# A seven-product down projection allowed earlier in the first pass, with new costs in the planner that orders all engines

## The chip, the cores and the metric

One core of a Trainium2 chip runs the whole kernel. The metric is the device time of one execution in microseconds (us). A core has five engines that run side by side and wait for each other through semaphores: TensorE (PE in the profile, its weight loads PEld), VectorE (DVE), ScalarE (ACT), GpSimd (POOL) and SyncE (SP), which here only issues DMAs. SBUF is the on-chip memory, PSUM the banks that TensorE writes into.

## The reference

The input x has 8192 tokens of 448 features. The reference normalizes each token, sends the result down two branches, and joins them:

```python
    x = A_x
    xn = _layernorm(x, axis=-1)
    s = _A_ref(xn, A_w1, A_b1, A_w2, A_b2)
    g = _silu(_B_ref(xn, B_w_gate, B_w_up, B_w_down))
    return x + s * g
```

Branch A (`_A_ref`) is a real FFT over the 8192 tokens, a two-layer complex MLP on each frequency in four blocks of 112 features, a soft threshold, and the inverse FFT. Branch B (`_B_ref`) is a gated feed-forward network (FFN), `(_gelu(x @ w_gate) * (x @ w_up)) @ w_down`, with 448 features in, 1792 hidden and 448 out. All arithmetic has to hold float32-like accuracy, so the kernel splits each float32 operand into two float16 halves, high and low, and uses three matmuls (high x high, high x low, low x high) for one product.

## The kernel before

**Two passes of the FFN.** The 14 hidden blocks of 128 do not fit at once. A first pass (p = 0) takes blocks 0 to 7, a second (p = 1) blocks 8 to 13. Each pass runs over 16 chunks of 512 tokens (`NG`, `ffn`, `chunk`). Chunks 0 and 1 of the first pass are done in a plain way at the start (`plain`, `down`). The partial result of the first pass goes to DRAM as `prt` and is read back in the second.

**One chunk.** `chunk(p, i)` works on pairs of hidden blocks, four pairs in the first pass and three in the second. Gate and up projection of a pair use a Strassen-like scheme of seven products (`unit`, `product`, steps a1 to a7) with operands that were combined before: the token side is prepared by stage 1 (`chunk1`, `factors`), goes through DRAM as `xts` and comes back transposed as `xta` and `xtb`; the weight side is prepared by `gu_comb`. After them comes the down projection, in one of two forms:

- *Plain* (`down`, `ended`): for each of the four tiles of 128 tokens and each of the 8 hidden blocks three matmuls of 448 columns, 96 in all; one ACT eviction per token tile.
- *Seven products* (`down2`, `prod2`, `add2`, `ended2`): the same Strassen-like scheme on pairs of hidden blocks, halves of the features and pairs of token tiles: seven products for each of four pairs, in two halves, with three matmuls of 224 columns each. It needs sums and differences of the hidden values (`sums` inside `unit`), and a right-hand side of combined down weights. Evictions add into a tile that an earlier product has filled. Half of this chunk's down projection is issued inside the next chunk (`state["tail"]`), between its first products.

The flag `state["seven"]` chooses. It is set at the start of a chunk, once and for good, when `state["products"]` is there and, in the first pass, the chunk number is at least 9. Setting it starts `factors_in(0)`, which loads the combined down weights from DRAM (`dsp`) into `dw`, into parts of `wt` and into `state["right"]`.

**Where "products" comes from.** `weights()` runs the preparation of weights in the background: first the blocks of the first pass (`gu_loads`, `gu_block`, `gu_split`, then `gu_combs`), then `room()`, which gives back the buffers, then four tasks `factor0(j)`. Each loads 256 rows of the down weights into the one remaining buffer of the ring `WS`, builds seven combinations and stores them to `dsp[0]`. `state["products"]` is set 3 us after the last of them is planned to land. Then follow the blocks of the second pass (`far_tile`), its down weights and the weights of the MLP (`prep_mlp`).

**Phases beside the FFN.** Stage 1 of the FFT is in `chunk1`, which also makes the FFN's input; its chunks are released every `DT` us from `T1` on (`first`). Phase 2 (`phase2`, `group`) starts when stage 1 and all preparation are done, and spreads 64 groups up to `END2` = 1450 us. Phase 3 (`phase3`, `load3`, `tiles3`) does the last inverse step and the output. It starts when phase 2 has stored everything. For chunks whose gate was stored to DRAM by then (`gsp`), it loads the gate into one of two buffers `g2`, multiplies, adds x and stores the output. Chunks that come later take the inverse step themselves (`gate_bank`, `gate`).

**The order.** Nothing here is ordered by hand, and nothing by the compiler. The kernel contains a planner, `Pace`: every step is a Python generator, a model clock decides which generator continues, and the instructions go into the engines' queues in that order. `cost` gives a duration for each instruction, `start` the earliest time, `note` and `ready` what was read and written when. `STEPS` corrects the model by time: in each row stand the start time, a limit for engines that are busy ahead (used by `clear`), an allowance for loads and a factor on durations. On the chip the queues run in that order and wait on semaphores, so a wrong cost does not make a wrong result, but a queue that stands behind the wrong instruction. Two helpers choose an engine: `Either` takes DVE or POOL (`B`), ACT or POOL (`A`), by which ends first; `calm` lets background work wait until the engine is free.

A duration on DVE or POOL gets longer in the model when the other one holds the SBUF port that both use (`shares`, `port`). Before, only the instruction planned later is lengthened.

The line L235 of the profile is the helper that issues every instruction, so tiles, and not lines, tell the work apart: `bd` holds down products, `bx` and `by` the others; `h`, `gl`, `u`, `left` the hidden values; `g` the tiles of phase 3.

Of the kernel before, what the change touches and what calls it, by code (L numbers as in the profile page):

```python
# [42 lines left out]
STEPS = ((0, 2.75, 0.05, 1), (100, 2.5, 0.15, 1.05), (175, 3, 0.2, 0.98), (250, 2.75, 0.05, 1), (325, 2.5, 0.05, 1), (400, 3.0, 0.1, 1.04), (475, 2.5, 0.05, 1), (550, 3.5, 0.05, 1), (700, 3.25, 0.3, 1), (775, 3.0, 0.3, 0.995), (850, 2.75, 0.05, 0.96), (925, 2.75, 0.05, 1.06), (1150, 2.5, 0.15, 0.995), (1450, 3, 0.1, 0.99), (1525, 2.75, 0.05, 1.02))  # L43
# [6 lines left out]
class Event:  # L50
    def __init__(self):
        self.done, self.waiting = False, []


class Pace:
# [4 lines left out]
    def __init__(self):  # L60
        self.now, self.last, self.n, self.heap = 0.0, 0.0, 0, []
        self.free, self.seen, self.dma = {"SP": 0.7, "ACT": 0.7, "DVE": 0.7, "POOL": 0.7, "PE": 1.0}, {}, 1.75
        self.port = {"DVE": [], "POOL": []}
        self.due = {"DVE": [], "ACT": []}
        self.late = False

# [72 lines left out]
    def ready(self, ap, write, engine):  # L139
        name, lo, hi = self.region(ap)  # L140
        return max((t + 0.12 for a, b, w, t, e in self.seen.get(name, ())
                    if (write or w) and e != engine and a < hi and lo < b), default=0.0)

    def note(self, ap, write, t, e):
# [4 lines left out]
        was.append((lo, hi, write, t, e))  # L149

    def quiet(self, ap):
        return max((x[3] for x in self.seen.get(ap.tensor.name, ())), default=0.0)

    def start(self, e, out, ins):
        outs = [out] if out.space != bass.MemoryType.DRAM else []
        ins = [i for i in ins if i.space != bass.MemoryType.DRAM]
        return outs, ins, max([self.now, self.free.get(e, 0.0)] + [self.ready(i, False, e) for i in ins]
                              + [self.ready(o, True, e) for o in outs])

    def issue(self, e, op, out, ins, run):  # L160
        outs, ins, start = self.start(e, out, ins)
        if e == "SP" or op == "dma_start":
            size = (outs or ins)[0].nbytes()
            self.dma = max(self.dma, start) + size / (320e3 if start > 10.0 else 400e3)
            if start < 10.0:
                self.free[e] = start + 0.46
                end = self.dma + 0.9
            elif op == "dma_start_transpose":
                self.free[e] = start + 1.15 + size / 380e3
                end = max(self.free[e] + 2.6, self.dma + 1.5)  # L170
            else:
                self.free[e] = start + 0.5
                end = max(start + 2.2 + size / 240e3, self.dma + 1.5) + (self.step(start)[1] if outs and start > 100.0 else 0.0)
        else:
            end = start + self.cost(e, op, start, out, ins) * (1.0 if e == "PE" else self.step(start)[3])
            self.free[e] = end
            if self.shares(e, op, out, ins):
                self.port[e] = self.port[e][-11:] + [(start, end)]
        for i in ins:
            self.note(i, False, end, e)  # L180
        for o in outs:
            self.note(o, True, end, e)
# [15 lines left out]
    def shares(self, e, op, out, ins):  # L198

        n, sb, psum = self.wide(out, ins)  # L200
        return e == "POOL" or e == "DVE" and n >= 32 and not psum and (sb >= 2 or op == "tensor_scalar" and sb > 0)

    def cost(self, e, op, start, out, ins):
# [8 lines left out]
        if e == "POOL":  # L212
            t = 0.7 if n < 8 and op == "tensor_tensor_pow" else 0.2 + 0.0023 * n
        elif n < 32:
            return 0.17
        elif psum or sb < 2 and op != "tensor_scalar":
            half = psum == len(ins) == 1 and op == "tensor_copy" and ins[0].dtype == F16
            return 0.14 + (0.00054 if half else 0.00107) * (n + 60 * (extra > 0))
        else:
            t = (0.12 + 0.00112 * n if sb >= 2 else 0.15 + 0.0008 * n) + 0.06 * (extra > 0)  # L220
        other, ahead = ("POOL", 0.15) if e == "DVE" else ("DVE", 0.0)
        return t + max([b - start - ahead for a, b in self.port[other] if a <= start < b] + [0.0])
# [17 lines left out]
class Either:  # L240
# [5 lines left out]
    def __getattr__(self, op):  # L246
        def call(out, *args):
# [4 lines left out]
            return getattr(self.engines[ends[1] + self.by < ends[0]], op)(out, *args)  # L252
# [249 lines left out]
def afno_geglu_kernel(ctx, tc, x, gu, raw, wd, mlp, b1, b2, c_m, c_mt, c_small, c_rows, out):  # L502
# [126 lines left out]
    WS = ring(wp, [128, SL * 128], F32, "wst", 3)  # L629
# [197 lines left out]
    T1, DT = 85.0, 34.5  # L827


    def gu_loads(fs, again):  # L830
        for f in fs:
            t = yield from WS.get()
            if f < 4 and not again:
                yield 2.5 + 2.5 * f

            n = (SL if again else 8) * 128
            Q.dma_start(t[:, 0:n], (raw if again else gu)[f])
            EV["wst", f, again] = t if again else t[:, 0:n].rearrange("p (s c) -> p s c", s=8)
# [51 lines left out]
    def gu_block(b):  # L890
# [23 lines left out]
        for i in range(n):  # L914
# [5 lines left out]
            WS.put(t)  # L920
# [941 lines left out]
    def chunk(p, i):  # L1862
        nf = PF[p][1]
        nxt = (p, i + 1) if i + 1 < NG else ((1, 0) if p == 0 else None)
        if "products" in state and "seven" not in state and (p or i >= 9):
# [577 lines left out]
    def begin():  # L2443

        w = yield from WS.get()
# [12 lines left out]
        Q.dma_start(w[:, 0:8 * 128], gu[0][:, 0:8 * 128])  # L2458
# [14 lines left out]
        keep(13, 512)  # L2473
# [6 lines left out]
        t = EV["wst", 0, 0] = w[:, 0:8 * 128].rearrange("p (s c) -> p s c", s=8)  # L2480
# [109 lines left out]
        WS.put(w)  # L2590
# [92 lines left out]
    def weights():  # L2683

        near = range(PF[0][1])
        t = yield from WS.get()
        Q.dma_start(t[:, 0:8 * 128], gu[1][:, 0:8 * 128])
        EV["wst", 1, 0] = t[:, 0:8 * 128].rearrange("p (s c) -> p s c", s=8)
        pace.spawn(gu_loads(near[2:], 0))
# [4 lines left out]
        combs = pace.spawn(gu_combs(near))  # L2694
# [3 lines left out]
        for f in near:  # L2698
# [61 lines left out]
```

## Time and profile before

| | us |
|---|---|
| median of the runs shown (3) | 1761.59 |
| lowest and highest of them | 1759.45 and 1762.22 |
| the profiled execution's own time | 1758.21 |
| its span, first to last instruction | 1756.4 |
| granted TensorE clock, mean | 0.993 |

A row of the view of windows has a stretch of the span, its length, and then for each engine the time in which it was busy and the number of instructions. A row of the timeline has the start, the duration (for merged instructions from the first start to the last end), the engine, the operation, what it writes and reads, the shape and the count; in brackets stands the idle time before it and what ended it. Matmuls overlap, so their rate is read from start to start. A row of a group has the count, the total busy time and the mean duration in ns.

### The profile page before, as it was taken

The numbers are of one execution on the slowest core, as the hardware profiler recorded it, in microseconds if no ns is written. First come the engines' busy times: TensorE is split into PE (matmuls) and PEld (weight loads), VectorE is DVE, ScalarE is ACT, GpSimd is POOL, SyncE is SP. The second block draws the span as 40 slices with busy tenths as digits, with TensorE's granted clock in tenths as the row PEclk, the third lists the DMA queues.
The fourth block names the chain that finished last, engine by engine and source line by source line (L and its number), as shares of the span: only waits on it lengthen the run. The fifth ranks groups of instructions, "written<-read, shape, count | busy, mean of one in ns | idle before, by whom it ended". The sixth has DMA issues, their size and how long they took to land.

```text
span 1756.4 us, 40962 instructions
## 1 busy us (share of the span) xinstructions
PE 1715.7 (98%) x15645; PEld 1435.9 (82%) x15645; DVE 1418.7 (81%) x2606; ACT 1113.9 (63%) x2279; POOL 751.5 (43%) x1083
## 2 busy tenths in 40 slices
PE   8998999999999999999999999999999999999997
PEld 4445677777777998999999989999899989889886
DVE  7898797777778877788887778888888887787787
ACT  6566676576676566778777666777676666333333
POOL 2277675566554564344333344432233432222222
PEclk9999999999999999999999999999999999999999
DMA  6428888887678653253445775445555545999996
GB/s 212 146 83 277 247 258 267 227 249 206 195 246 232 168 124 83 60 121 93 107 110 180 191 171 123 119 109 133 136 131 139 132 100 131 302 292 301 274 311 224
DMA packets 438308, 316.62 MB, mean 180 GB/s; under 512 B 305792, under 2 KB 409600, under 8 KB 436320
## 3 DMA queue, kind: packets, MB, share of 16 engines
q1 hardware_dynamic: 437824, 313.99, 63.6%
q8 instruction: 122, 2.00, 0.5%
q14 instruction: 74, 0.61, 0.1%
q10 hardware_dynamic: 288, 0.03, 0.0%
HBM read 137.93 MB, written 108.25 MB: 140 GB/s over the span
## 4 chain that ended last, share of the span: by engine, by line
PE 84%; DVE 7%; DMA 3%; ACT 3%; issue 2%; SPq 1%; POOL 1%; DVEq 0%; ACTq 0%; POOLq 0%
PE bd L235 34%; PE bx L235 29%; PE by L235 21%; DVE wt L235 1%; DVE u L235 1%; SPq L235 1%; DVE h L235 1%; DMA wst<-in_gu 1%; DMA prt<-th 1%; DVE va L235 1%; DMA xtb<-xts 1%; ACT h L235 1%; DVE o L235 0%; DMA vt<-va 0%; ACT o L235 0%
## 5 line engine op out<-in xcount | busy, mean ns | idle before, releaser
L235 PEld LDWEIGHTS <-wt 128*128 128x128 f16 x9142 | 887.2, 98 | 173.8 <-issue 19.4
L235 PE MATMUL bx<-xta,wt 128*128 128x256 f16 (+1 forms) x2819 | 355.5, 276 | 3.5 <-DMA xta<-xts 2.5
L235 PEld LDWEIGHTS <-h 128*128 128x128 f16 x2711 | 258.8, 98 | 73.5 <-DVE h L235 1.5
L235 PE MATMUL by<-xtb,wt 128*128 128x256 f16 x2080 | 255.7, 273 | 2.4 <-DVE by L235 1.3
L235 PE MATMUL bd<-dw,h 128*128 128x448 f16 (+1 forms) x1536 | 243.2, 306 | 0.0
L235 PE MATMUL bx<-xtb,wt 128*128 128x256 f16 x1248 | 153.2, 273 | 2.4 <-DVE v L235 2.3
L235 POOL TENSOR_TENSOR wt<-wt 128x256 f32<-128x256 f32 x81 | 63.0, 778 | 209.8 <-DVE wt L235 198.7
L235 PE MATMUL by<-xta,wt 128*128 128x256 f16 (+1 forms) x899 | 126.4, 285 | 2.7 <-ACT wt L235 1.9
L235 DVE TENSOR_TENSOR by<-bx,u 128x512 f32<-128x512 f32 x104 | 72.3, 695 | 43.4 <-PE bx L235 36.3
L235 ACT ACTIVATE u<-by,fc 128x512 f32<-128x512 f32 (+1 forms) x118 | 73.5, 635 | 47.9 <-PE by L235 47.0
L235 PE MATMUL bd<-dw,wt 128*128 128x224 f16 (+1 forms) x816 | 98.2, 264 | 3.6 <-DVE left L235 3.2
L235 PE MATMUL bx<-left,wt 128*128 128x256 f16 x816 | 100.0, 273 | 0.3 <-ACT by L235 0.3
L235 ACT COPY u<-by 128x512 f32<-128x512 f32 x104 | 60.7, 583 | 51.0 <-PE by L235 50.4
L235 ACT CAST h<-wt 128x512 f16<-128x512 f32 (+1 forms) x128 | 68.5, 536 | 36.1 <-DVE wt L235 29.1
L235 DVE TENSOR_TENSOR v<-bx,u 128x512 f32<-128x512 f32 x104 | 71.1, 684 | 16.1 <-PE bx L235 15.2
L235 DVE SCALAR_TENSOR_TENSOR left<-bd,ms,left 128x448 f32<-128x448 f32 x96 | 64.2, 678 | 22.5 <-PE bd L235 22.0
L235 ACT COPY by<-bx 128x512 f32<-128x512 f32 x104 | 60.1, 578 | 32.9 <-PE bx L235 32.6
L235 POOL TENSOR_TENSOR t<-h 112x256 f32<-112x256 f32 (+1 forms) x36 | 30.0, 832 | 114.3 <-ACT h L235 93.1
L235 PE MATMUL bd<-w2t,wn 113*128 113x112 f16 (+1 forms) x1152 | 78.1, 212 | 0.7 <-DVE wn L235 0.3
L235 PE MATMUL bd<-wt,h 128*128 128x224 f16 x603 | 72.2, 259 | 0.8 <-DVE h L235 0.7
L235 DVE SCALAR_TENSOR_TENSOR u<-by,fc,u 128x512 f32<-128x512 f32 (+1 forms) x86 | 55.4, 658 | 21.5 <-PE by L235 11.9
L235 PEld LDWEIGHTS <-wn 113*128 113x128 f16 (+1 forms) x1152 | 69.1, 97 | 3.8 <-POOL wn L235 0.6
(275 smaller groups left out, 3707.9 us busy)
## 6 DMA issues: line engine op xcount, KB each, us to landing
xts<-sx SPq DMA_DIRECT2D x32, 480.0 KB, 4.1
x<-in_x SPq DMA_DIRECT2D x17, 896.0 KB, 6.6
wst<-in_raw SPq DMA_DIRECT2D x14, 1088.0 KB, 7.0
t<-ysb SPq DMA_DIRECT2D x64, 224.0 KB, 3.5
prt<-th SPq DMA_DIRECT2D x64, 224.0 KB, 3.3
vt<-va SPq DMA_DIRECT2D x256, 56.0 KB, 2.1
left<-prt SPq DMA_DIRECT2D x64, 224.0 KB, 3.8
u<-t SPq DMA_DIRECT2D x32, 448.0 KB, 5.7
```

The costliest lines, as they stand in the source:

```text
L235: return self.pace.issue(self.name, kind, out, ins, lambda: fn(out, *args, **kw))
```

## The change

The condition for the seven-product form reads 2 in place of 9:

```diff
-        if "products" in state and "seven" not in state and (p or i >= 9):
+        if "products" in state and "seven" not in state and (p or i >= 2):
             state["seven"] = True
             pace.spawn(later(lambda: factors_in(0)), pace.now + 2.0)
```

The planner's model of the two engines with a common port becomes mutual. An instruction that takes the port now also pushes back those of the other engine that were planned to begin later (`push_on`), with the times that were noted for their operands:

```diff
+    def push_on(self, e, start, end):
+
+        by, before = None, 0.0
+        for k, (a, b, marks) in enumerate(self.port[e]):
+            if a > start:
+                by = end - (0.15 if e == "DVE" else 0.1) - a if by is None else by - max(0.0, a - before)
+                if by <= 0.0:
+                    return
+                self.port[e][k], before = (a + by, b + by, marks), b
+                for x in marks:
+                    x[3] += by
+        if by is not None:
+            self.free[e] += by
...
+            end = start + self.cost(e, op, start, out, sb) * by
+            self.free[e] = end - OVER[e]
+            if self.shares(e, op, out, sb):
+                self.port[e] = self.port[e][-11:] + [(start, end, marks := [])]
+                self.push_on("POOL" if e == "DVE" else "DVE", start, end)
```

Other costs of the model change too. The delay from an instruction's end to a waiting engine is now given by engine (`LATE`: PE 0.2, ACT, DVE and POOL 0.045, SP 0.04; before 0.12 for all), and instructions of one engine overlap a little (`OVER`). A DMA costs 0.6 us of its queue and its size at 330 GB/s, or 210 where the pieces are under 512 bytes, plus 1.7; at most eight are in flight from SP. POOL's durations have new terms:

```diff
-            t = 0.7 if n < 8 and op == "tensor_tensor_pow" else 0.2 + 0.0023 * n
+            if n < 8:
+                t = 0.35 + 0.19 * n if op == "tensor_tensor_pow" else 0.25
+            elif sb < 2:
+                t = 0.18 + 0.00085 * n
+            else:
+                t = 0.18 + 0.0019 * n if out.dtype == F16 else 0.17 + 0.00217 * n
```

`STEPS` has rows every 10 to 25 us where it had 15, and a fifth column, a bias in us for the choice of `Either` between its two engines. `T1` goes from 85 to 84 and `DT` from 34.5 to 34. `END2` and `END3` stay.

At the start, the three buffers for raw weights become one tile `raws`, and the first eight weight tiles of 1024 columns lie two to a buffer (`near`), so that the first six can be loaded without waiting; tiles 6 and 7 wait until tiles 0 and 1 have been read:

```diff
+    raws = wp.tile([128, 3 * SL * 128], F32, name="raws")
+    whole = [raws[:, SL * 128 * k:SL * 128 * (k + 1)] for k in range(3)]
+    near = [whole[f // 2 % 3][:, 1024 * (f % 2):1024 * (f % 2) + 1024] for f in range(8)]
+    WS = Slots(pace, [])
...
+            else:
+                t = near[f]
+                if f < 4:
+                    yield 2.5 + 2.5 * f
+                elif f > 5:
+                    yield ev("read", f - 6)
+                    yield pace.ready(t, True, None)
+            Q.dma_start(t, (raw if again else gu)[f])
```

A buffer is given to the second round of loads (`gu_combs`) when both tiles in it have been split. Of the matmuls on a tile of ones at the very start, which compute nothing that is used, there are 22 where there were 13:

```diff
-        keep(13, 512)
+        keep(22, 512)
```

125 lines of the change are left out of this document (74 added, 51 removed).

## The prediction

> **What bounds the kernel now.** I read the page first: its head and the line of busy shares.
>
> ```profile
> span 1756.4 us, 40962 instructions
> PE 1715.7 (98%) x15645; PEld 1435.9 (82%) x15645; DVE 1418.7 (81%) x2606; ACT 1113.9 (63%) x2279; POOL 751.5 (43%) x1083
> ```
>
> TensorE is busy for 1715.7 of 1756.4 us, so 40.7 us of its time is idle. Next I cut the span into its stages with the view of windows (columns: stretch, length, busy time of PE, PEld, DVE, ACT and POOL with instruction counts, granted clock, DMA share, GB/s).
>
> ```profile
> 0.00:70.00 70.00, 59.97 (x298) 28.65 (x299) 52.83 (x106) 43.82 (x102) 18.14 (x39) 0.90 0.55 183
> 70.00:155.80 85.80, 82.53 (x407) 39.50 (x406) 77.92 (x160) 58.23 (x111) 54.17 (x84) 1.00 0.49 163
> 155.80:251.00 95.20, 92.17 (x726) 71.42 (x726) 76.98 (x144) 65.24 (x132) 62.14 (x108) 0.98 0.83 247
> 251.00:529.60 278.60, 278.12 (x2112) 205.93 (x2111) 214.04 (x406) 188.60 (x370) 166.42 (x314) 1.00 0.81 233
> 529.60:650.00 120.40, 120.40 (x1057) 102.32 (x1055) 97.97 (x208) 76.53 (x152) 66.62 (x115) 1.00 0.69 176
> 650.00:1490.00 840.00, 828.28 (x8731) 763.30 (x8730) 685.44 (x1247) 583.09 (x1243) 314.32 (x353) 1.00 0.50 124
> 1490.00:1746.00 256.00, 253.30 (x2317) 224.12 (x2315) 207.51 (x329) 96.42 (x169) 68.77 (x71) 1.00 0.91 290
> 1746.00:1756.40 10.40, 0.94 (x10) 0.69 (x8) 5.96 (x12) 1.93 (x4) 0.94 (x1) 0.68 0.40 132
> ```
>
> From 251 to 650 us TensorE idles 0.5 us in all: there the time is the matmul work alone, and a matmul saved is time saved, if nothing behind it gives it back. The idle time lies in the head (10.0 + 3.3 us), around the start of chunk 2 (3.0), in the second phase (840.0 - 828.28 = 11.7), in the third phase (2.7) and behind the last matmul (9.5). The third phase has a second nearly full resource: DMA at 0.91.
>
> **Matmuls saved per chunk.** The timeline gives the spacing of both forms, start to start: the old down projection (448 columns) at the end of chunk 3, the seven-product one (224 columns) in chunk 10.
>
> ```profile
> 263.32 9.81 PE L235 MATMUL bd<-dw,h 128*128 128x448 f16 x51
> 272.97 1.47 PE L235 MATMUL bx<-xta,wt 128*128 128x256 f16 x12
> ```
>
> ```profile
> 650.89 1.31 PE L235 MATMUL bd<-dw,left 128*128 128x224 f16 x12
> 652.04 1.31 PE L235 MATMUL bd<-wt,left 128*128 128x224 f16 x12
> ```
>
> Old: (272.97 - 263.32) / 51 = 0.189 us, times 4 tokens x 8 blocks x 3 = 96 matmuls: 18.2 us a chunk. New: (652.04 - 650.89) / 12 = 0.096 us, times 7 products x 4 pairs x 2 halves x 3 = 168: 16.1 us. So 2.0 us a chunk.
>
> **How many chunks.** The condition now says chunk 2, but "products" must also be set, and that comes 3 us behind the last of four factor tasks of the first pass, which share one buffer.
>
> ```profile
> 172.54 0.50 SPq L235 DMA_DIRECT2D wst<-in_down  x1
> ...
> 248.74 0.55 SPq L235 DMA_DIRECT2D dsp<-wo  x1
> ```
>
> ```profile
> dsp<-wo SPq DMA_DIRECT2D x7, 784.0 KB, 4.7
> ```
>
> The first task loads at 172.5, the fourth stores at 248.7 and lands 4.7 us later, so "products" is set at about 256. Chunk 4 begins at 273.0 (the row above), 17 us behind the event. Chunk 3 began one period earlier, and the period is read from the loads of both chunks' inputs:
>
> ```profile
> 194.81 4.11 SPq L235 DMA_TRANSPOSE xta<-xts  x1
> ...
> 250.96 7.11 SPq L235 DMA_TRANSPOSE xta<-xts  x1
> ```
>
> 273.0 - 56.2 = 217, which is 39 us too early. The first condition to decide is therefore the products, not the number: chunks 4 to 8 change, five of the seven named. Gain: 5 x 2.0 = **-10.1 us**. Bounds: four chunks (-8.1) to seven (-14.1).
>
> **What the seven products add.** Per pair of blocks, seven sums or differences of 256 columns on DVE or POOL and three casts on ACT more than before; per chunk, three evictions on DVE that add to what is there. Rows of the same work in 529.6 to 1000 us:
>
> ```profile
> L235 DVE TENSOR_TENSOR u<-gl,u 128x256 f32<-128x256 f32 x25 | 14.0, 560 | 0.8 <-POOL gl L235 0.2
> ...
> L235 DVE SCALAR_TENSOR_TENSOR th<-bd,ms,th 128x448 f32<-128x448 f32 x14 | 9.5, 681 | 10.2 <-PE bd L235 10.2
> ```
>
> ```profile
> L235 POOL TENSOR_TENSOR gl<-u,gl 128x256 f32<-128x256 f32 x12 | 9.4, 785 | 12.0 <-DVE gl L235 11.5
> ```
>
> ```profile
> L235 ACT CAST h<-gl 128x256 f16<-128x256 f32 x56 | 22.7, 405 | 8.2 <-DVE gl L235 8.1
> ```
>
> That is 28 x 0.56 = 15.7 us if DVE takes all (22.0 if POOL does, at 0.785) plus 3 x 0.68 = 2.0, so about 18 us for the two engines, and 12 x 0.405 = 4.9 us for ACT, a chunk. The fullest period is chunk 3's end with the start of chunk 4, the emptiest with seven products is chunk 10:
>
> ```profile
> 251.00:307.70 56.70, 56.70 (x429) 41.47 (x428) 47.54 (x93) 39.32 (x78) 34.42 (x66) 1.00 0.90 266
> 583.20:632.60 49.40, 49.40 (x477) 45.95 (x475) 38.79 (x78) 32.22 (x66) 26.69 (x47) 1.00 0.53 141
> ```
>
> DVE and POOL hold 82 of 113 us there; with 18 they hold 100. I take **0** on the path. What hides it: the weight preparation and stage 1 yield to a busy engine, so they are pushed back and not the chunk's own steps. The last preparation, of the MLP weights, loads at 524, and the second phase first loads y at 655:
>
> ```profile
> L235 SPq DMA_DIRECT2D raw<-in_mlp x1: 373/373/373, 524.1 to 524.1; - x1
> ```
>
> ```profile
> 655.32 0.92 SPq L235 DMA_DIRECT2D y<-t  x2
> ```
>
> So 131 us of room. Without this cover it is the slower rival below.
>
> The Trainium skill, "SBUF — State Buffer", section "Who interferes with whom", says that a DVE instruction with two SBUF inputs and a GpSimd instruction that reads SBUF exclude each other for a whole instruction. By it the 18 us are one queue and not two, and moving some to POOL buys nothing. The trace bears it out in single rows: a DVE addition with a median of 624 ns has taken 1577 beside POOL (the fence on the third phase has the row). The sum is the same by the rule and without it, as long as the room lasts. By rows: over 251 to 529.6 DVE idles 64.6 us and five chunks add 90, so even if DVE takes it all, some 25 us of preparation move behind 530.
>
> The factors' loads (26 of them: 28 blocks of 224 columns, two halves, 128 rows, 2 bytes: 3.2 MB) move to about 275, onto the SP queue that also issues the chunks' inputs.
>
> ```profile
> 551.32 0.89 SPq L235 DMA_DIRECT2D dw<-dsp  x2
> ```
>
> Before, at 551, they cost PE nothing. At 275 DMA stands at 0.90 (row 251.00); at its 266 GB/s they take 12 us, and the products that read them come behind 307.7, where chunk 5's input is loaded. I take 0, at most +6 if they push that input back.
>
> **The head.** Six of the eight first weight tiles no longer wait for a free slot; 9 more warm-up matmuls are issued.
>
> ```profile
> 1.46 4.98 PE L235 MATMUL bx<-gl 128*128 128x512 f16 x13 [1.46 <-DVE gl L235]
> 8.74 0.22 PE L235 MATMUL bd<-ident,fx 128*2 128x128 bf16 x1 [2.31 <-DVE fx L235]
> ...
> 13.43 1.30 PE L235 MATMUL bx<-xs,m 128*128 128x448 f16 x3
> 14.53 1.55 PE L235 MATMUL by<-xta,wt 128*128 128x256 f16 x7
> ...
> 41.96 2.10 PE L235 MATMUL by<-xta,wt 128*128 128x512 f16 x7 [1.45 <-ACT wt L235]
> ...
> 155.81 2.71 PE L235 MATMUL bx<-xta,wt 128*128 128x256 f16 x12 [2.46 <-DMA xta<-xts]
> ```
>
> The gap of 2.3 us at 6.4 leaves the clock low: at 13.43 a 448 takes (14.53 - 13.43) / 3 = 0.37 us instead of 0.189. Nine matmuls more fill it and can save some 2 us; earlier weights can save most of the 1.5 us at 41.96 and like ones. But chunk 2 cannot start before its input:
>
> ```profile
> 144.41 3.98 SPq L235 DMA_DIRECT2D xts<-xs  x5
> 148.49 4.36 SPq L235 DMA_TRANSPOSE xta<-xts  x1
> ```
>
> The transpose follows the last store at once, and that store ends a chain of stage 1 on DVE (77.9 of 85.8 us busy), which starts only 1 us earlier (T1). So PE would reach 155.8 sooner and wait longer. I take **-1.5** (bounds 0 and -8.8: the head's 10.0 idle without the 1.46 and the 2.31, and the 2.46).
>
> **The new order.** Costs of the planner change for all engines, so every queue's order changes after the head. No row prices that. Of the 11.7 us idle in the second phase I take a quarter back, **-3**, as an estimate; bounds -9 and +9.
>
> **The tail.** The second phase aims at 1450 us as before, so the third begins near 1490 again, with chunk 10 and so 22 tiles that pass through two buffers of g2.
>
> ```profile
> L235 DVE TENSOR_TENSOR g<-g,x x34: 607/624/1577, 1507.0 to 1743.2; 128x448 f32<-128x448 f32 x34
> ...
> L235 SPq DMA_DIRECT2D out<-g x22: 332/357/543, 1515.4 to 1743.9; - x22
> ```
>
> ```profile
> 1742.76 2.46 PE L235 MATMUL bd<-u,mt 128*128 128x448 f16 x18 [0.96 <-DMA mt<-c_mt]
> ```
>
> They leave every (1743.9 - 1515.4) / 21 = 10.9 us, and the last one 2 us before the last matmul: this loop and the FFN end together. If the FFN comes 14.6 us ahead, the loop must be that much shorter to follow. DMA is at 0.91 over the stage and reaches 0.98 in its fullest part:
>
> ```profile
> 1540.00:1590.00 50.00, 50.00 (x460) 44.36 (x459) 42.80 (x69) 18.93 (x33) 14.88 (x15) 1.00 0.98 313
> ```
>
> At 0.98 throughout it could shrink by 256 x (1 - 0.91 / 0.98) = 18 us; if its two buffers set its pace, by nothing. So the price lies between 0 and +14.6. I take **+3**, nearer to the free end, since part of the loop's time is waiting for engines that the FFN then leaves.
>
> Sum: -10.1 - 1.5 - 3 + 3 = -11.6. The profiled execution took 1758.21 (span 1756.4 and 1.8 around it), which gives 1746.6; the median of the runs shown is 1761.59, 3.4 higher, and on that scale I forecast **1750.0**.
>
> **Rivals.**
> - *The third phase holds the end.* The loop of 10.9 us does not shorten, and all of what the FFN gains turns into waits of PE for u2, mt or g2 behind 1700. For it: DMA at 0.91 and the wait of 0.96 us. Against it: while it runs PE idles only 2.7 us. Time: 1761.6 - 1 = 1757 to 1761. Chance 0.20.
> - *Slower: DVE and POOL block each other in chunks 4 to 8.* Place: the seven sums of a pair, which the next chunk's down products wait for, and the buffers that they hold longer. Price: x per pair in 5 x 4 = 20 pairs; the gain of 11.6 is gone from x = 0.6 us, and it is slower by more than 3.5 from x = 0.75, about one POOL instruction (0.785) in the way each time. With 1 us: 1761.6 - 11.6 + 20 = 1770. For it: 100 of 109 us held, and the addition that took 1577 ns. Against it: 529.6 to 650 has seven products beside stage 1 with no idle PE. Chance 0.10.
> - *The head and the second phase gain as well.* Head -5.5, second phase -6, tail 0: -21.6, so 1740 (1733 to 1742). Chance 0.13.
> - *It does not do what it says:* "products" comes behind chunk 4's start, and chunk 5 is the first: 1752; or chunk 2 really is the first: 1746. Both lie inside the forecast's range.
>
> **Numbers.** Forecast, 1742 to 1757: 0.57. About 0.2%, 3.5 us, is what a measurement of this kernel can tell from no change, so faster means below 1758.1. Faster: 0.57 + 0.13 + a part (0.05) of the first rival = 0.75; same 0.14; slower 0.11. The range 1738 to 1762 leaves out the far end of the gain and the slower rival.
>
> **What would show it.** Five chunks more with 224-column down products, the first load of dw from dsp near 275 and not 160: step one. A PE idle still below 1 us between 251 and 530: the cover. The MLP weights loaded later than 524 but well before 655. PE waits around 155.8 as long or longer. The interval between the last out<-g and the last matmul: if PE waits there for DMA by 10 us, the first rival. It is wrong if the periods of chunks 4 to 8, read from the input loads (56.2 us for chunk 3), do not shorten by about 2 us.

## The result, and the profile after

The kernel after takes 1744.05 us (median of 4 runs, 1743.2 to 1746.5), the kernel before 1760.64 beside it (4 runs, 1759.45 to 1762.22). The ratio is 0.9908 with a 95% interval of 0.989 to 0.9925: about 16.6 us, or 0.9%, faster. The forecast was 1750.0 with a range of 1738 to 1762.

The profiled execution took 1743.2 us, 15.0 less than that of before. Its page begins:

```profile
span 1741.4 us, 41899 instructions
...
PE 1703.9 (98%) x16019; PEld 1468.9 (84%) x16019; DVE 1455.5 (84%) x2534; ACT 1122.8 (64%) x2303; POOL 984.6 (57%) x1346
```

There are 16019 - 15645 = 374 matmuls more. Five chunks with 168 in place of 96, and 9 more at the start, make 369, and 5 more were not traced: so five chunks changed their form. TensorE is busy for 11.8 us less and idle for 1741.4 - 1703.9 = 37.5 us in place of 40.7. The view of windows of the kernel after, with the stretches of before (the last one runs to the end):

```profile
0.00:70.00 70.00, 66.39 (x354) 32.47 (x355) 59.58 (x121) 50.21 (x112) 27.20 (x50) 1.00 0.61 212
70.00:155.80 85.80, 83.35 (x455) 44.05 (x453) 81.69 (x158) 59.72 (x116) 55.87 (x96) 1.00 0.61 180
155.80:251.00 95.20, 95.03 (x721) 69.96 (x719) 84.30 (x163) 69.05 (x138) 54.29 (x97) 1.00 0.91 263
251.00:529.60 278.60, 272.23 (x2500) 241.84 (x2499) 240.96 (x422) 188.00 (x388) 218.66 (x344) 1.00 0.75 213
529.60:650.00 120.40, 116.81 (x1080) 104.34 (x1078) 108.58 (x217) 81.53 (x168) 90.58 (x155) 1.00 0.66 173
650.00:1490.00 840.00, 833.87 (x8780) 768.33 (x8778) 686.40 (x1170) 584.57 (x1229) 440.66 (x513) 1.00 0.52 127
1490.00:1741.40 251.40, 236.25 (x2144) 207.96 (x2141) 194.04 (x289) 89.68 (x157) 97.34 (x96) 0.98 0.95 297
```

Length minus PE's busy time gives the idle time of each stretch:

| stretch | idle before | idle after | change |
|---|---|---|---|
| 0 to 251 (head, stage 1, chunks 2 and 3) | 16.3 | 6.2 | -10.1 |
| 251 to 650 (chunks 4 to 8) | 0.5 | 10.0 | +9.5 |
| 650 to 1490 (second phase) | 11.7 | 6.1 | -5.6 |
| 1490 to the end | 12.2 | 15.2 | +3.0 |
| sum | 40.7 | 37.5 | -3.2 |

So the net change of 3.2 us in idle time is made of four changes that partly cancel, two of each sign. The biggest gain and the biggest loss are both in places where the forecast had little or nothing (1.5 us and 0). POOL shows how far the order has moved: it holds 984.6 us in place of 751.5, most of the difference in the second phase (440.66 against 314.32) and in chunks 4 to 8.

A second reading goes by marks that both kernels have. The loads of the chunks' inputs in the timeline of the kernel after (chunks 2, 4 and 8):

```profile
132.41 6.18 SPq L288 DMA_TRANSPOSE xta<-xts  x1
...
235.70 4.20 SPq L288 DMA_TRANSPOSE xta<-xts  x1
...
453.93 4.34 SPq L288 DMA_TRANSPOSE xta<-xts  x1
```

and that of chunk 8 before (those of chunks 2 and 4, at 148.49 and 250.96, stand in the prediction):

```profile
474.37 4.12 SPq L235 DMA_TRANSPOSE xta<-xts  x1
```

The last matmuls of the FFN's down projection, before and then after, there with the last matmuls of all:

```profile
1746.49 0.45 PE L235 MATMUL bx<-wt,h 128*128 128x224 f16 x3
```

```profile
1726.19 0.45 PE L288 MATMUL bx<-wt,h 128*128 128x224 f16 x3
...
1729.86 1.29 PE L288 MATMUL bd<-u,mt 128*128 128x448 f16 x6 [0.38 <-DVE g L288]
```

Chunk 4's input is 15.3 us earlier, chunk 8's 20.4, the FFN's end 20.3, and the end of the span 15.0. The lead is there before the first seven-product chunk begins, and another 5.1 come by the input of chunk 8. Behind that no more is won on balance: the lead is 17.1 us at the input of chunk 12 (685.35 before, 668.30 after) and 20.3 again at the FFN's end. The end of the span keeps 15.0 of it. Most of the missing 5.3 is a change of order and no loss: in the kernel after, 21 matmuls of the inverse step stand behind the FFN's last one, where there were none before. The last matmul of all ends 15.8 us earlier (at 1746.94 before, 1731.15 after).

The marks that the prediction named: the first load of the combined factors, and the second phase's first y (timeline of after):

```profile
261.71 1.32 SPq L288 DMA_DIRECT2D dw<-dsp  x2
...
682.69 0.90 SPq L288 DMA_DIRECT2D y<-t  x2
```

and the load of the MLP weights, from the view of one tile:

```profile
L288 SPq DMA_DIRECT2D raw<-in_mlp x1: 1167/1167/1167, 544.4 to 544.4; - x1
```

The factors come at 262 and not at 160, so the event "products" decides and chunk 4 is the first. The background work did yield: the MLP weights load 20 us later and the second phase starts 27 us later than before. And yet PE idles 10.0 us from 251 to 650. The three largest of the six rows in the view of PE's waits there (us in total, times, longest):

```profile
PE bx L288 <- DVE v L288: 4.9, 8, 1.1
PE bx L288 <- ACT by L288: 1.7, 2, 1.2
PE bx L288 <- ACT gl L288: 1.2, 1, 1.2
```

These are short waits of the gate and up products for their chains on DVE and ACT, none above 1.2 us; the three other rows come to 2.0 us.

### The profile page after: what moved, and what is told of

It is laid out like the page before. It is cut to its first block, busy times and chain, and to the rows that moved or that the text cites. A ratio compares the mean times of both kernels' runs of the same rounds, so it can differ in the third digit from the quotient of the medians.

```text
span 1741.4 us, 41899 instructions
## 1 busy us (share of the span) xinstructions
PE 1703.9 (98%) x16019; PEld 1468.9 (84%) x16019; DVE 1455.5 (84%) x2534; ACT 1122.8 (64%) x2303; POOL 984.6 (57%) x1346
## 4 chain that ended last, share of the span: by engine, by line
PE 52%; DVE 6%; POOL 3%; DMA 2%; ACT 1%; issue 1%; SPq 0%; DVEq 0%; ACTq 0%; POOLq 0%
PE bd L288 23%; PE bx L288 16%; PE by L288 12%; DMA xtb<-xts 1%; DVE wn L288 1%; POOL sx L288 1%; POOL wt L288 1%; DMA x<-in_x 1%; DVE wt L288 1%; DVE h L288 1%; DVE gl L288 1%; POOL h L288 0%; DVE va L288 0%; DVE u L288 0%; DMA t<-u 0%
## 5 line engine op out<-in xcount | busy, mean ns | idle before, releaser
L288 PE MATMUL bd<-dw,h 128*128 128x224 f16 (+1 forms) x1266 | 170.6, 280 | 0.1
L288 POOL TENSOR_TENSOR wt<-wt 128x256 f32<-128x256 f32 x106 | 83.5, 788 | 130.6 <-DVE wt L288 126.1
L288 PE MATMUL bd<-wt,h 128*128 128x224 f16 x693 | 84.7, 260 | 3.7 <-POOL h L288 2.3
L288 PEld LDWEIGHTS <-left 128*128 128x128 f16 x864 | 81.4, 98 | 4.2 <-issue 1.7
```

Of the source, the lines that this page charges most:

```text
L288: return self.pace.issue(self.name, kind, out, ins, lambda: fn(out, *args, **kw))
```

## The experiments

Two theories were set against each other. **A**: the sums that the change adds lie on PE's path and make the waits of chunks 4 to 8, while the products and the head give the gain. **B**: the waits, and much of the gain, belong to the order that the planner's table `STEPS` gives; an order that differs at all has other waits. Either can hold in part.

### The condition put back, and the condition alone

The kernel after with the old condition:

```diff
-        if "products" in state and "seven" not in state and (p or i >= 2):
+        if "products" in state and "seven" not in state and (p or i >= 9):
```

> The changed kernel with the condition back at chunk 9, all else as changed. If five chunks save 2.0 us each of matmul time and lose some of it to waits: the matmul time of the span grows by 10.1 us; theory A (the waits of 9.5 us that the changed kernel shows between 251 and 650 us come from the added sums): they fall back to about 0.5 and the time stays within 2 us of the changed kernel's 1744. Theory B (those waits come from the new order itself): they stay and the time rises by 8 to 10 us to about 1753.

It took 1765.48 us (1764.08 to 1768.68), ratio to before 1.0027 [1.0016, 1.0037], so 21.4 us more than after, which neither theory had expected. PE is busy for 1719.7 us, 15.8 more than after, where 10.1 were expected. Up to chunk 4 PE's order is that of after, and the input of chunk 4 is loaded at 236.22 us (after: 235.70); so the lead up to there does not need the seven products. Its windows:

```profile
251.00:529.60 278.60, 272.98 (x2081) 202.82 (x2080) 221.84 (x421) 186.04 (x360) 187.56 (x330) 1.00 0.80 223
529.60:650.00 120.40, 117.94 (x1063) 102.92 (x1062) 86.99 (x144) 67.36 (x138) 74.46 (x116) 1.00 0.63 172
```

PE idles 5.6 + 2.5 = 8.1 us there with none of the added sums: nearly the 10.0 of the kernel after. This speaks against A. But the edit also made a new order from chunk 4 on, so the 21.4 us are not the worth of the seven products.

The other way round, the kernel before with only the condition changed from 9 to 2:

> The kernel before with the condition at chunk 2 alone; planner, steps and head as before. Theory A: the matmul time falls by 10.1 us, waits of several us appear between 273 and 530 where there were 0.5, and the time falls by less than 10, to 1752 to 1758. Theory B: no waits appear, and the time falls by 10 to about 1750.

It took 1796.15 us (1795.29 to 1796.66), 1.0201 [1.0183, 1.022]: 35 us slower than before, although it saves the same matmuls; neither theory had that. Its factors load at 277.5, so here too chunk 4 is the first. PE idles 74.7 us, of them 11 in chunks 4 to 8, 25 in the second phase and 22.5 behind 1490. The costs lie mostly where no sum was added. PE's busy time does not fall but rises, from 1715.7 to 1718.8 us, at a granted clock of 0.988 in place of 0.993.

One cost shows here that the kernel after escapes. The 26 loads of the factors hold SP's queue from 277.5 to 299.5 us, the input of chunk 5 is loaded only at 314.67 (before: 307.66), and PE waits for it:

```profile
325.19 2.72 PE L235 MATMUL bx<-xta,wt 128*128 128x256 f16 x12 [3.35 <-DMA xta<-xts]
```

### The head

The kernel before with the new weight buffers and 22 warm-up matmuls, and all else as before:

```diff
+    near = [whole[f // 2 % 3][:, 1024 * (f % 2):1024 * (f % 2) + 1024] for f in range(8)]
...
-        keep(13, 512)
+        keep(22, 512)
```

> The kernel before with the eight early weight tiles loaded without waiting for slots and with 22 matmuls on the tile of ones; planner, steps and condition as before. If the head's gain is the early weights and the clock: PE idle before chunk 2 falls from 13.3 us to about 7 and chunk 2 begins some 8 us sooner, with the end 5 to 9 us earlier, 1752 to 1756. If chunk 2's input sets that start (as the prediction had it), chunk 2 begins at 154 or later and the end moves by under 2 us.

It took 1757.31 us (1754.76 to 1760.39), 0.9981 [0.997, 0.9992], 4.0 us less than the 1761.28 of before beside it. Its inputs of chunks 2 and 4, and two of its windows:

```profile
141.38 4.38 SPq L235 DMA_TRANSPOSE xta<-xts  x1
...
251.85 4.27 SPq L235 DMA_TRANSPOSE xta<-xts  x1
```

```profile
0.00:155.80 155.80, 145.53 (x751) 71.13 (x752) 134.84 (x274) 104.86 (x214) 73.81 (x133) 0.99 0.57 185
155.80:251.00 95.20, 88.82 (x684) 67.69 (x682) 75.25 (x140) 62.66 (x125) 54.80 (x98) 0.96 0.76 224
```

The input of chunk 2 comes 7.1 us earlier, its first matmul 4.2 (151.60 in place of 155.81), and the input of chunk 4 comes 0.9 later: PE idles 10.3 us before 155.8 in place of 13.3, and 6.4 instead of 3.0 behind it. Left in an order that was not made for it, the earlier head gives its gain back at once. The 4.0 us at the end are not this gain: PE idles 8.7 us in the second phase in place of 11.7, and 9.9 behind 1490 in place of 12.2. The run lies between its two expectations.

The kernel after with 13 warm-up matmuls:

```diff
-        keep(22, 512)
+        keep(13, 512)
```

> The changed kernel with 13 matmuls on the tile of ones in place of 22. If the warm clock matters: the 448-column matmuls near 13 us take 0.37 us again, the first 70 us do 2 to 3 us less work and the time rises by 2 to 3 us to about 1747. If the later waits swallow that, it stays within 1 us of 1744.

It took 1745.47 us (1744.27 to 1745.73), 0.9911 [0.9896, 0.9926]. That is 1.4 us more than after by the medians and 1.1 by the profiled spans, between the two expectations, and the intervals of the two ratios overlap. So the nine matmuls are worth about a microsecond, hardly more than the scatter of the runs, and the rest of the lead does not come from them.

### The planner's model

The kernel after without the call that makes the port's collisions count both ways:

```diff
-                self.push_on("POOL" if e == "DVE" else "DVE", start, end)
```

> The changed kernel without the call of push_on: the planner counts a collision of DVE and POOL only against the instruction planned later, as before. If counting both ways is what makes the order good, the time rises by clearly more than in the nudged kernel, with more waits of PE for DVE and POOL in 251 to 650 (20 us or more) and in the second phase. If not, it lies with the nudged one.

It took 1809.41 us (1807.97 to 1810.89), 1.0263 [1.0248, 1.0279], 65 us more than after; PE idles 84.9 us, of them 30.7 from 251 to 650 (after: 10.0) and 18.3 in the second phase (after: 6.1). By its own expectation counting both ways matters, since the nudged kernels of the next part lose only 22. But the table had been fitted with the call in place and was left as it is; what a table fitted without the call would give was not run.

### How much hangs on the table

One factor of the table was moved by 0.2%, a change in the model's durations that no instruction notices; only the order differs. Twice in the kernel after, at row 100 (1.01 to 1.012) and at row 150:

```diff
-STEPS = (... (150, 3.0, 0.2, 1.05, 0.0), ...)
+STEPS = (... (150, 3.0, 0.2, 1.052, 0.0), ...)
```

> The changed kernel with one planner factor nudged by 0.2% (1.01 to 1.012 for 100 to 125 us): the same work, no cost that means anything is changed, but the order of the queues comes out differently from about 100 us on. If the order as such is worth little, the time stays within 3 us of 1744 and the waits between 251 and 650 us stay near 10. If the table of steps is fitted to one order, the time rises by 8 to 25 us, as it did with the condition at 9 in the changed kernel (1765.5) and with the condition at 2 in the old one (1796).

> The kernel after with one factor of the planner's table, that of DVE, ACT and Pool operations from 150 us on, at 1.052 in place of 1.05; the same instructions in another order from 150 us on. Theory B (the gain of the whole hangs on the order that the table was fitted to): 10 to 25 us slower than after, 1754 to 1769, with the waits spread over the stages behind 155. Theory C (the first nudge, at 100 us, hit a weak place, and the order is otherwise worth little): within 4 us of after, 1740 to 1748.

and twice in the kernel before, at row 0 (1 to 1.002) and at row 100:

```diff
-STEPS = (... (100, 2.5, 0.15, 1.05), ...)
+STEPS = (... (100, 2.5, 0.15, 1.052), ...)
```

> The kernel before with one planner factor nudged by 0.2% (1 to 1.002 for 0 to 100 us). If the order as such is worth little: 1758 to 1764, waits between 251 and 650 us about 0.5. If its table is fitted to one order: waits of 5 us or more appear between 251 and 650, and the time is 1768 to 1785.

> The kernel before with the factor from 100 us on at 1.052 in place of 1.05; the same instructions in another order. Theory B: 8 to 20 us slower than before, 1769 to 1781, as its other nudge was 12. Theory C: within 4 us of before, 1757 to 1765.

| kernel | us, median (range) | ratio to before [95%] | PE idle, profiled |
|---|---|---|---|
| after, row 100 | 1766.14 (1764.62 to 1777.73) | 1.0023 [1.0012, 1.0035] | 59.9 |
| after, row 150 | 1766.30 (1764.27 to 1770.82) | 1.0037 [1.0025, 1.0049] | 56.5 |
| before, row 0 | 1773.09 (1772.57 to 1773.41) | 1.0057 [1.0042, 1.0072] | 51.6 |
| before, row 100 | 1771.99 (1768.77 to 1776.25) | 1.0068 [1.0046, 1.0089] | 49.4 |

All four are slower than the kernel that they came from: the kernel after by 22 us, that of before by 11 to 12. So the third possibility, that the first nudge had hit a weak place (C), falls with the second. Both kernels sit in fitted orders, and the new one has more to lose. (The idle time is that of the profiled execution, which in three of the four is the slowest run. In the first kernel it lies 11.6 us above the median, so the stages are read from others.) Rows 251 to 650 of the kernel after nudged at row 150, then of before nudged at row 100:

```profile
251.00:529.60 278.60, 262.08 (x2343) 227.20 (x2341) 248.17 (x416) 186.24 (x385) 231.56 (x361) 0.99 0.75 213
529.60:650.00 120.40, 113.03 (x1046) 101.57 (x1045) 101.44 (x196) 76.32 (x154) 90.01 (x148) 0.99 0.63 168
```

```profile
251.00:529.60 278.60, 275.23 (x2085) 202.74 (x2083) 221.21 (x411) 185.01 (x361) 161.89 (x297) 1.00 0.80 227
529.60:650.00 120.40, 115.89 (x988) 95.51 (x986) 92.16 (x190) 72.18 (x142) 58.75 (x102) 1.00 0.58 161
```

The first idles 23.9 us there, the second 7.9. DVE and POOL together hold 671 us of twice 399 in the first and 534 in the second: with the sums added, a chance order costs more. All runs in an order that was not fitted agree: without the sums in this stretch PE idles there 3.6 us (the head alone), 7.9, 8.1 (the condition put back) and 8.8; with them 11.2 (the condition alone), 23.1, 23.9 and 30.7 (collisions counted one way).

Nudged against nudged, the new kernel leads by 1772.5 - 1766.2 = 6.3 us, somewhat over a third of the 16.6 between the fitted ones. These are two orders each, so it is a rough figure. The lead at the input of chunk 4 lasts better: it is loaded at 242.75 and 239.75 us in the two nudged kernels after and at 251.75 and 258.77 in those of before, 14 us apart on average (the nudge at row 150 changes the order only from about 200 us on). What a chance order loses, the new kernel loses mostly behind that point.

### The sums, in an order that stays

Two runs change the work on DVE and POOL and leave the order of every queue as it is. The first adds three additions of 256 columns on DVE to each pair in chunks 4 to 8, unknown to the planner:

```diff
+            if seven and p == 0 and i < 9:
+                for _ in range(3):
+                    nc.vector.tensor_add(gl[:, 512:768], gl[:, 0:256], gl[:, 256:512])
```

> The kernel after with three more additions of 256 columns on DVE behind every pair's hidden tiles in the first-pass chunks 4 to 8, unknown to the planner, so that every queue's order stays as it is: 60 operations, by the rows of 0.45 to 0.55 us for such an addition without Pool beside it some 27 us of DVE. They write a scratch region that is overwritten at once, so the values stay. Theory A (the sums that the change adds lie on the path, and they make the 6.4 + 3.6 us that PE idles in 251 to 650): the same work once more costs most of what it takes, 8 to 27 us more than the kernel after, 1752 to 1771. Theory B (the sums are covered by work that yields to them, and PE's waits there come from the order): below 4 us more, 1744 to 1748, and PE idle in 251 to 650 within 3 us of 10.

The second does three of the eight sums of a pair on 8 columns, so that most of these three is left out, and plans them as if they were whole:

```diff
+            pace.narrow = p == 0 and i < 9
             B.tensor_sub(a21, a11, a21)
             B.tensor_sub(a11, x, a11)
...
             B.tensor_sub(a12, a12, a11)
+            pace.narrow = False
```

> The kernel after with three of the eight sums of every pair in the first-pass chunks 4 to 8 done on 8 columns in place of 256, planned as if they were whole, so that every queue's order stays as it is: 60 operations of 0.65 to 0.9 us fall to about 0.2, some 25 us less on DVE and 7 less on Pool. It leaves that part of the sums out. Theory A (the sums lie on the path): PE idle in 251 to 650 falls from 10.0 to 5 or below and the time by 4 to 10 us, to 1734 to 1740. Theory B (the order makes the waits): within 3 us of the kernel after, 1741 to 1747, idle there 8 to 10.

More work took 1774.11 us (1772.86 to 1775.93), 1.0076 [1.0058, 1.0094]; less took 1740.62 (1739.03 to 1741.09), 0.9886 [0.9871, 0.9901]. The first is 30 us above the kernel after, more than the 8 to 27 that A expected. Windows of the first and then of the second:

```profile
251.00:529.60 278.60, 251.31 (x2227) 217.41 (x2226) 241.66 (x436) 168.33 (x346) 194.33 (x309) 0.98 0.68 193
529.60:650.00 120.40, 113.36 (x1036) 99.99 (x1036) 108.19 (x213) 81.08 (x165) 89.12 (x140) 1.00 0.61 168
```

```profile
251.00:529.60 278.60, 275.96 (x2539) 245.53 (x2538) 231.60 (x432) 191.28 (x396) 207.89 (x349) 1.00 0.76 217
529.60:650.00 120.40, 116.75 (x1080) 104.31 (x1079) 108.27 (x214) 81.96 (x170) 89.44 (x152) 1.00 0.64 171
```

The 60 additions lengthen DVE's busy time by 1482.9 - 1455.5 = 27.4 us, and the span by 32.7: PE's idle time from 251 to 650 rises from 10.0 to 34.3 us, and PE is busy 8.3 us longer with the same matmuls. Nothing is won back later: the second phase idles 6.7 us as against 6.1. In this stretch work that the order was not made for has hardly any cover: of the 27.4 us, 24.3 turn into idle time of PE. The additions stand in front of the sums in DVE's queue, so the sums come later by their length. POOL's busy time stays (984.6 to 984.1 us), so they do not cost by lengthening POOL's instructions.

The other direction is far flatter. DVE's busy time falls by 11.5 us and POOL's by 15.3 (1455.5 to 1444.0 and 984.6 to 969.3). The median is 3.4 us lower and the profiled span 2.1; the intervals of the ratios of both kernels overlap, so the gain in time is hardly clear of noise. The idle time is: it falls from 10.0 to 6.3 us, while the two other kernels with this same order up to 650 us (13 warm-up matmuls above, the second phase aimed earlier below) idle 10.7 and 10.5. It lies between what A (5 or below) and B (8 to 10) expected. So a part of the waits, some 3.7 us, belongs to these three sums; the other 6.3 were not traced to any one operation, and 8.1 are there without the sums in another order.

### The tail

The kernel after with the second phase aimed 15 us earlier:

```diff
-    END1, END2, END3 = T1 + NG * DT + 12.0, 1450.0, 1730.0
+    END1, END2, END3 = T1 + NG * DT + 12.0, 1435.0, 1730.0
```

> The changed kernel with the second phase aimed at 1435 in place of 1450 us, so that the third starts some 15 us sooner; the order up to about 690 us is unchanged. If the loop of the third phase holds the end by the 5 us by which its last tile comes behind the last FFN matmul: its last tile comes before that matmul and the time falls by 3 to 6 us to about 1740. If the end is set by the amount of DMA and matmuls, it stays within 2 us; if the denser second phase costs waits, it rises.

It took 1745.21 us (1743.4 to 1748.16), 0.9901 [0.9884, 0.9918]: no change that is clear of noise. The view of the tile `out` gives the 22 stores of the third phase's loop, with first and last start, for the kernel after and then for this one; its last FFN matmul follows:

```profile
L288 SPq DMA_DIRECT2D out<-g x22: 332/357/688, 1516.1 to 1737.7; - x22
```

```profile
L288 SPq DMA_DIRECT2D out<-g x22: 338/356/1409, 1497.5 to 1732.9; - x22
```

```profile
1737.52 0.45 PE L288 MATMUL bx<-wt,h 128*128 128x224 f16 x3
```

The loop now starts 18.6 us earlier and ends 4.8 earlier, and the FFN ends 11.3 later (1737.52 against 1726.19). What one gains the other loses, and the end stays: PE idles 10.1 us behind 1490 in place of 15.2, and 10.3 in the denser second phase in place of 6.1. That loop and FFN share PE and DMA would explain it; no run separates the two.

No run with the whole computation was faster than the kernel after.

## Why the prediction was right, and where it was not

The sign and the range held, and the time lies 6 us below the forecast. But the sum came near by luck as much as by its terms, as misses partly cancelled: in idle time of PE the head gave 8.6 us more than its term and the second phase 2.6 more, and chunks 4 to 8 took 9.5 that stood at 0.

- **Seven products, -10.1: right.** Five chunks by the count of matmuls, chunk 4 first, the factors at 262 (the forecast said near 275). Of the 11.8 us less of busy PE, 10.1 are this term by its own working; no run shows it by itself, since the run with the condition put back has another order too. The nine warm-up matmuls add 1.8 us (6.80 against 4.98), so 3.5 us less come from elsewhere, most likely from the higher clock (0.90 to 1.00 in 0 to 70).
- **The cover, 0: right in what yields, wrong in what it buys.** The preparation went back 20 us, within the 131 us of room. But the mark set for this step, idle below 1 us from 251 to 530, failed: it was 6.4, and 10.0 up to 650. The step that failed took room for the background as room for the chunk's own chain. Some 3.7 us of the idle time went when three of the eight sums were narrowed; how the rest divides between the sums and the order is open. In the queues nothing yields: what is planned yields beforehand, and the run with unplanned additions paid 32.7 us for 27.4. The prediction's test of the periods passed in sign only: from chunk 4's input to chunk 8's, (453.93 - 235.70) / 4 = 54.6 us against (474.37 - 250.96) / 4 = 55.9, so 1.3 shorter and not 2.0 (1.6 against the 56.2 of chunk 3).
- **The factors' loads, 0:** no wait for them is among PE's waits from 251 to 650; right for this order. With the condition alone, in the order of before, they did push an input back, and PE waited 3.35 us.
- **The head, -1.5: the term that was mis-sized most.** PE's idle time before 251 fell by 10.1 us and the input of chunk 4 came 15.3 earlier. The failed step is "The transpose follows the last store at once, and that store ends a chain of stage 1 on DVE (77.9 of 85.8 us busy), which starts only 1 us earlier (T1)". I read a chain that an order had made as a bound of the engine. The chain came 16.1 us earlier (148.49 to 132.41), with DVE at 59.58 of the first 70 us where it was at 52.83, and POOL at 27.20 where it was at 18.14. Chunk 2 begins at 143.22 in place of 155.81, and the wait for its input, which the prediction expected as long or longer, is gone. The head's edits alone bring 7.1 of the 16.1 and lose that by chunk 4; so the rest needs the new costs, their table or the earlier release of stage 1 (`T1`, `DT`), which no run took apart.
- **The new order, -3: right in sign.** The second phase, for which it was meant, idles 5.6 us less. No row had priced it, so this is luck. Part of the 9.5 us more in chunks 4 to 8 is the order too. The bounds of -9 to +9 were too narrow as a measure of what an order is worth: a factor moved by 0.2% costs 11 to 22 us.
- **The tail, +3: right in idle time** (12.2 to 15.2), but by another mechanism, so by luck. The term priced a loop that cannot follow the FFN. The loop followed: it sped up to (1737.7 - 1516.1) / 21 = 10.55 us a tile, so it was not held by its two buffers alone, and behind 1700 PE waits for it only once, for 0.38 us. The largest pieces of the idle time are now two waits near the FFN's end, of 1.44 and 2.30 us, for hidden values from ACT and POOL (rows in the last section; why these were late was not traced), and the stretch behind the last matmul, 10.2 us in place of 9.5.

Of the rivals, the one in which the third phase holds the end fell: it had the FFN's gain turn into waits of PE for the loop behind 1700, and there is one such wait, of 0.38 us, while the span ends 15.0 us earlier. The slower one, DVE and POOL blocking each other in chunks 4 to 8, had the right place, but stayed below its point: 9.5 us over 20 pairs is 0.48 us a pair, and it decided from 0.6. In the kernel after nudged at row 150, (23.9 - 0.5) over 20 pairs is 1.2, and that kernel is slower than before. Whether it is the blocking or the mere length of the work was not separated; in the run with more additions POOL's busy time did not grow, which there speaks for the length. The rival in which the head and the second phase gain as well described the gains better than the forecast did (-5.5 and -6, measured -10.1 and -5.6 in idle time); it lacked the waits of chunks 4 to 8.

What stays open: how the lead of 15.3 us at chunk 4 divides between the weight buffers, the costs, the table and the release of stage 1; and what the seven products would be worth in a fitted order without the rest.

## What to carry to other kernels

Where a program issues work in a fixed order that a model has fitted, an edit is not judged by undoing it: the order changes with it, and that alone cost 11 to 22 us here, more than most terms of the sum. Add or narrow work in a way that leaves the order alone, and nudge the order without changing the work; the two together tell a cost from a lucky order. Free time on an engine is cover only for work that the order was made for, and a chain that ends just in time in a trace may be early or late by choice of the order, so it is no bound before its engine is shown to be full.

## What the hardware showed that was not expected

A short stall of TensorE can cost more than its length. In the run with more additions a wait of 2.86 us is followed by slow matmuls (timeline of PE):

```profile
303.74 2.40 PE L288 MATMUL bd<-dw,left 128*128 128x224 f16 x12 [2.86 <-ACT th L288]
...
319.83 1.31 PE L288 MATMUL bd<-wt,left 128*128 128x224 f16 x12
```

Twelve of 224 columns take 2.40 us and, 16 us later, 1.31. The view of windows shows the granted clock at half:

```profile
304.00:308.00 4.00, 4.00 (x21) 2.82 (x20) 2.86 (x5) 1.38 (x4) 2.18 (x3) 0.50 0.71 197
```

The matmuls from 303.74 to 310.26, where the full rate is back, take 6.5 us; at its spacings (0.096, 0.109 and 0.189 us for 224, 256 and 448 columns) they would take 3.6. So the stall of 2.86 us cost 2.9 more. Much the same happens in the tail of the kernel after, where the slow stretch begins somewhat behind the waits:

```profile
1714.87 0.37 PE L288 MATMUL bd<-wt,h 128*128 128x224 f16 x2 [1.44 <-ACT h L288]
1717.53 1.13 PE L288 MATMUL bd<-wt,h 128*128 128x224 f16 x10 [2.30 <-POOL h L288]
...
1719.33 2.45 PE L288 MATMUL bd<-dw,wt 128*128 128x224 f16 x12
...
1722.46 1.31 PE L288 MATMUL bd<-dw,wt 128*128 128x224 f16 x12
```

Such stretches go with the 8.3 us more of busy PE in the run with more additions, beside 24.4 more of idle; its granted clock is 0.94 from 297 to 358.5 us. In the kernel after nudged at rows 100 and 150 PE is busy 12.2 and 8.5 us longer than in the kernel after, with the same 16019 matmuls.

The Trainium skill, "TensorE: Matmul & The Clock Gate", Part 1, says that TensorE falls back to half its clock after at least one idle window of about 3.4 us. The half rate agrees with the clock of 0.50; the length does not, as a single gap of 2.86 us was enough here, and by the measurement even a stall below 3 us can cost about twice its length.

A gap of such a length does not always do it. A shorter one in the kernel after nudged at row 100 is followed by slow matmuls, a longer one than that in the kernel before with the head alone is not:

```profile
317.84 2.09 PE L288 MATMUL bx<-xta,wt 128*128 128x256 f16 x10 [2.05 <-ACT by L288]
319.73 2.18 PE L288 MATMUL bd<-left 128*128 128x224 f16 x12
```

```profile
587.51 1.47 PE L235 MATMUL bx<-xtb,wt 128*128 128x256 f16 x12 [2.71 <-DVE v L235]
588.82 1.31 PE L235 MATMUL bd<-dw,h 128*128 128x224 f16 x12
```

The fourteen traces of this case give a count, from 60 to 1735 us, of gaps of TensorE with no other gap above 0.25 us in the 8 us before and the 4 us behind. Counted is whether the matmuls in the 4 us behind the gap lost more than 0.7 us against the full rate. Between 1 and 2 us, 1 of 82 gaps did that; between 2 and 3 us, 8 of 16; above 3 us, all 14, and the loss was mostly about 1.5 us. One of the 8 is the gap of 2.46 us at 155.81 that the prediction shows, behind which 12 matmuls of 256 columns take 2.71 us where they take 1.47 at 272.97.

In the head the same shows from the other side. The first matmuls of the kernel after, and then of that kernel with 13 warm-up matmuls, in which the queues of the other engines have the same order:

```profile
1.45 6.80 PE L288 MATMUL bx<-gl 128*128 128x512 f16 x22 [1.45 <-DVE gl L288]
8.68 0.22 PE L288 MATMUL bd<-ident,fx 128*2 128x128 bf16 x1 [0.43 <-DVE fx L288]
8.84 0.39 PE L288 MATMUL bx<-gl 128*128 128x256 f16 x2
...
12.52 0.74 PE L288 MATMUL bx<-xs,m 128*128 128x448 f16 x3
```

```profile
8.64 0.27 PE L288 MATMUL bd<-ident,fx 128*2 128x128 bf16 x1 [2.41 <-DVE fx L288]
8.84 0.61 PE L288 MATMUL bx<-gl 128*128 128x256 f16 x2
...
13.33 1.30 PE L288 MATMUL bx<-xs,m 128*128 128x448 f16 x3
```

With the gap cut from 2.41 to 0.43 us, two matmuls of 256 columns take 0.39 us at 8.84 where they took 0.61, and three of 448 take 0.74 us at 12.52 where they took 1.30 at 13.33. The rate is up from the first real work on; at the end of the kernel this is worth about the microsecond that the run with 13 showed.
